# Seventeen bursts of score tiles in place of eighteen, and the last out product in two column halves

## The chip, the core and the metric

The kernel runs on one NeuronCore of a Trainium2 chip. Its engines run side by side, each through its own list of instructions in order: TensorE (PE; its weight loads are listed apart as PEld), VectorE (DVE), ScalarE (ACT), GpSimd (POOL) and SyncE (SP), which here only issues DMAs. Results of TensorE go to PSUM, eight banks of 512 f32 columns by 128 partitions. An engine that needs another's result, or a bank that another still reads, waits on a semaphore. The metric is the device time of one execution in microseconds; a lower one is better. The profile is of one execution, times in it are counted from the start of its span.

## What is computed

Attention with a sigmoid in place of the softmax, and behind it a two-layer network with the SiLU function. Inputs q, k and v have 8 batches, 12 heads, 448 rows and 64 columns; w_in is 768 x 2048, w_out 2048 x 768.

```python
scores = q @ k.T / sqrt(64) - log(448)
attn = sigmoid(scores) @ v            # for each batch and head
x = attn.transpose(0, 2, 1, 3).reshape(3584, 768)
h = x @ w_in
out = (h * sigmoid(h)) @ w_out        # 3584 x 768, float32
```

## The kernel before

**Groups and tiles.** Four heads of one batch make a group g, so a batch has three groups and there are 24. A group has seven score tiles (`scores`, L216): TensorE multiplies k and q into a double bank of PSUM (`psc`, four matmuls a tile), and ScalarE turns the 128 x 896 tile into `attnT` with one sigmoid (L230). When a group's seven tiles are through, `values` (L238) multiplies them with v on TensorE (28 matmuls into `pav`, L254), and VectorE moves the two results to `xT` (L265).

**Stages.** After a first stretch the program goes through pairs of batches, m = 0 to 3. For each pair there is a stage of out products (`sets`, L570: gTr, the hidden layer of pair m, times w_out) and a stage of hidden products for the next pair (`h_pair`, L360). Both use Strassen-like sums, seven products in place of eight. In the first three out stages the score tiles of pair m + 1 are put between the out products, 42 tiles (six groups) a stage; the fourth has none.

**An out set** (`out_set`, L485) makes two blocks of 128 rows: seven products of eight matmuls (384 columns each, L502), each into one bank `po` and then taken out by VectorE: L513, L517, L523, L526, L529, L534 with L535, L539 in that order. Sums of operands (`S`, L510 to L518) are VectorE's as well. The function is a generator and yields after each matmul; one yield is called a step here, so a product has eight steps and a set 56. In the eighth step of a product the instructions that take it out are issued. Stages m = 0 and 2 have three sets (168 steps), m = 1 and 3 four. Results are stored from `osb` with DMAs on SyncE's queue; in the last set of the program (`last`) the stores go by column halves, and some on ScalarE's queue: the left halves, then those on the right, two DMAs of 64 rows each.

**Banks.** In the first three out stages there are three double banks, taken in turn by score tiles and by `values` (L64 with 3), and two single ones for `po`. In the last stage, four single ones.

**The order of work in an out stage** is written out by hand (L765 to L786). A first number of steps is run (`FIRST_DENSE`), then a list of bursts: each has a size, the score tiles that it issues one after the other, and a count, the out steps that follow. With a burst's tiles goes one `values` if a group is complete (`burst`, L741). After the tiles, and once more in the middle of the count, `rows_if_any` (L589) puts in what waits for a place: a copy for the transpose of later q or k rows, with its DMA on SyncE's queue, or one of four sums of `xT` (`x_sums`, L343) that the hidden stage needs. At the end of the list the remaining steps of the stage run, ScalarE loads the SiLU table, and the hidden stage begins; its first two products stand ahead of the last group's `values`. At the start of an out stage ScalarE loads the sigmoid table (L771).

```python
FIRST_DENSE = 14
THREE_SETS = [(2, 8), (2, 9), (3, 13)] + [(2, 2), (2, 9), (3, 13)] * (2 * NQ - 1)
...
for size, count in bursts:
    burst(n, size)
    n += size
    rows_if_any(own, nc.vector.tensor_copy)
    for i in range(count):
        next(stream)
        if i == count // 2:
            rows_if_any(own, nc.vector.tensor_copy)
```

NQ is 3, so this list has 18 bursts: 42 tiles and 150 steps. With the 14 first ones 164 steps of 168 are through when it ends.

Of the kernel before, what the change touches and what calls it, by code (L numbers as in the profile page):

```python
# [17 lines left out]
def kernel(  # L18
# [9 lines left out]
    nc = tc.nc  # L28
# [8 lines left out]
    NQ = NPAIR // 2  # L37
# [3 lines left out]
    NO2 = DMODEL // 2  # L41
    NQB = NQ * B
    NHC = NFC // 2
# [20 lines left out]
    def banks_for_attention(doubles):  # L64
        psum.close()
        banks.clear()
        bufs_of.update(double=doubles, single=NBANK - 2 * doubles)
        for name, bufs in bufs_of.items():
            taken[name] = 0
            new_pool(name, bufs)  # L70
# [7 lines left out]
    def banks_for_h():  # L78
        doubles = [[2 * i, 2 * i + 1] for i in longest_idle("double")]
        ring[:] = sum(doubles[:-2], [])  # L80
        ring.extend(2 * bufs_of["double"] + i for i in longest_idle("single"))
        ring.extend(sum(doubles[-2:], []))
        psum.close()
        banks.clear()
        new_pool("any", 1)
        for i in range(NBANK):
            banks[i] = banks["any"].tile([P, 512], F32, tag=f"any{i}", name=f"any{i}")

    def one_bank(name):
        if "any" in banks:  # L90
            ring.append(ring.pop(0))
            return banks["any"].tile([P, 512], F32, tag=f"any{ring[-1]}", name=name)
        taken["single"] += 1
        return banks["single"].tile([P, 512], F32, tag="single", name=name)
# [265 lines left out]
    def h_pair(m, last_values):  # L360
# [97 lines left out]
    wq = [  # L458
        [w_out_sb[:, r * NHC : (r + 1) * NHC, c * NO2 : (c + 1) * NO2] for c in range(2)]
        for r in range(2)  # L460
    ]
# [23 lines left out]
    def out_set(a1, rows1, a2, rows2, last=False):  # L485
        lo, hi = slice(0, NHC), slice(NHC, NFC)
        osb = [p3.tile([P, DMODEL], F32, tag="osb", name="osb") for _ in range(2)]
        c11, c12 = (osb[0][:, nh * NO2 : (nh + 1) * NO2] for nh in range(2))
        c21, c22 = (osb[1][:, nh * NO2 : (nh + 1) * NO2] for nh in range(2))
        m1 = cpool.tile([P, NO2], F32, tag="m1", name="m1")  # L490
        sg = [cpool.tile([P, NHC, P], F16, tag=f"S{i}", name=f"S{i}") for i in range(1, 5)]

        def store(rows, o, cols, engines):
            for at, (row, eng) in enumerate(zip(rows, engines)):
                eng.dma_start(row[:, cols], o[at * HP : (at + 1) * HP, cols])

        left, right, whole = slice(0, NO2), slice(NO2, DMODEL), slice(0, DMODEL)

        def product(a, w):
            po = one_bank("po")  # L500
            for fc in range(NHC):
                nc.tensor.matmul(  # L502
                    po[:, :NO2], a[:, fc, :], w[:, fc, :], start=(fc == 0), stop=(fc == NHC - 1)
                )
                if fc < NHC - 1:
                    yield 163
            return po[:, :NO2]

        add, sub = nc.vector.tensor_add, nc.vector.tensor_sub
        add(sg[0], a2[:, lo], a2[:, hi])  # L510
        sub(sg[1], sg[0], a1[:, lo])
        po = yield from product(a1[:, lo], wq[0][0])
        (act_copy if last else nc.vector.tensor_copy)(m1, po)  # L513
        sub(sg[2], a1[:, lo], a2[:, lo])
        yield 163
        po = yield from product(a1[:, hi], wq[1][0])
        add(c11, po, m1)  # L517
        sub(sg[3], a1[:, hi], sg[1])  # L518
        if last:
            store(rows1, osb[0], left, (nc.sync, nc.sync))  # L520
        yield 163
        po = yield from product(sg[1], tw[2])
        add(c12, po, m1)  # L523
        yield 163
        po = yield from product(sg[2], tw[3])
        add(c22, po, c12)  # L526
        yield 163
        po = yield from product(a2[:, hi], tw[4])
        sub(c21, c22, po)  # L529
        if last:  # L530
            store(rows2, osb[1], left, (nc.sync, nc.scalar))
        yield 163
        po = yield from product(sg[0], tw[1])
        add(c22, po, c22)  # L534
        add(c12, po, c12)  # L535
        store(rows2, osb[1], right if last else whole, (nc.sync, nc.sync))
        yield 163
        po = yield from product(sg[3], wq[1][1])
        add(c12, po, c12)  # L539
        if last:  # L540
            store(rows1, osb[0], right, (nc.sync, nc.scalar))
        else:
            store(rows1, osb[0], whole, (nc.sync, nc.sync))
        yield 163

    by_h1 = {3: 6, 6: 7, 9: 8}
    early = [h_unit(0, fc) for fc in range(2)]
# [22 lines left out]
    def sets(m):  # L570
        for g in range(0, NCH - 1, 2):
            step = out_set(
                block(m, g), row_blocks(m, g), block(m, g + 1), row_blocks(m, g + 1)
            )
            for i, ns in enumerate(step):
                if m == 0 and g == 0 and i in (10, 14):
                    next(sums)
                if m == 0 and g == 0 and i in (20, 28, 36, 44):
                    next(in_sums)
                yield ns  # L580
        if m % 2 == 1:
            g = NCH - 1
            yield from out_set(
                kept, row_blocks(m - 1, g), block(m, g), row_blocks(m, g), m == B // 2 - 1
            )
# [3 lines left out]
    def rows_if_any(before, copy):  # L589
        if sums_of_x and next(sums_of_x[0], "end") == "end":  # L590
            sums_of_x.pop()
        if later and later[0][0] < before:
            g, name = later.pop(0)
            dma_transpose(g, name, copy)
            if name == "q":
                behind_rows(g, before)
# [49 lines left out]
    def after_values(g):  # L646
        if g == 0:
            load("v", 3)
            load_w_in(2)
            load_w_in(3)  # L650
        elif g == 1:
            load("v", 4)
            load_w_out(0, 0)
            load_w_out(0, 1)
        elif g == 2:
            load("v", 5)
            load_w_out(1, 0)
            load_w_out(1, 1)
            load("kq", 6)
            load("kq", 7)  # L660
        elif g + 3 < NQB:
            load("v", g + 3)
        if g >= 2 * NQ and g % (2 * NQ) == 2 * NQ - 2:
            sums_of_x.append(x_sums(g // (2 * NQ), 0, NQ - 1))
# [76 lines left out]
    def burst(n, size=2):  # L741

        new = units[n : n + size]
        for u in new:
            scores(*u)
        with_values = values_if_any()
        for g, ch in new:
            if ch == NCH - 1:
                waiting.append(g)
                if 9 <= g + 3 < NQB:  # L750
                    later.extend(((g + 3, "k"), (g + 3, "q")))
        return with_values
# [9 lines left out]
    for _ in stream:  # L762
        pass

    FIRST_DENSE = 14  # L765
    THREE_SETS = [(2, 8), (2, 9), (3, 13)] + [(2, 2), (2, 9), (3, 13)] * (2 * NQ - 1)
    FOUR_SETS = [(size, {2: 6, 3: 16}[size]) for size in (3, 3, 3, 2, 3, 2, 3, 3, 2, 3, 3, 2, 3, 2, 3)]
    FOUR_SETS.append((2, 10))
    for m in range(B // 2 - 1):
        banks_for_attention(3)  # L770
        nc.scalar.activation(warm, bias_s, AF.Sigmoid)  # L771
        stream = sets(m)
        for _ in range(FIRST_DENSE):
            next(stream)
        bursts = FOUR_SETS if m % 2 else THREE_SETS
        assert sum(size for size, _ in bursts) == 2 * NT_B
        own = 2 * NQ * (m + 2)
        n = 2 * NT_B * (m + 1)
# [8 lines that stand above are left out]
        assert not sums_of_x  # L787
        nc.scalar.activation(warm, bias_s, AF.Silu)
        for _ in stream:
            pass  # L790
        (g,) = waiting
        waiting.clear()
        banks_for_h()

        def last_values():
            values(g)
            after_values(g)
            for _ in x_sums(m + 1, NQ - 1, NQ):
                pass
            nc.gpsimd.tensor_copy(gate, tx[m + 1, 4][:1, NQ - 1, :1])  # L800

        for i, _ in enumerate(h_pair(m + 1, last_values)):
            if i % 8 == 7:
                rows_if_any(NQB, nc.gpsimd.tensor_copy)
# [33 lines left out]
```

## Time and profile before

| | us |
|---|---|
| time, median of 3 runs (lowest to highest) | 365.48 (365.35 to 365.48) |
| the profiled execution: its time | 365.46 |
| its span | 363.5 |
| out stage of m = 0 | 74.2 to 120.6 |
| out stage of m = 1 (four sets) | 154.0 to 209.6 |
| out stage of m = 2 | 242.8 to 289.2 |
| out stage of m = 3 (no score tiles) | 322.8 to the end |

The time is the span and what lies around it. Busy times of engines are sums of their instructions; matmul ends in the profile are modelled, so starts of matmuls are the better mark. The granted clock of TensorE is full from the first microseconds on. In the timeline a line gives start, length, engine, line of the program, what is written from what, and how many instructions are merged; in square brackets stands how long the engine was idle before it and for whom. "SPq" and "ACTq" are the queues on which these engines issue DMAs.

### The profile page before, as it was taken

The numbers are of one execution on the slowest core, as the hardware profiler recorded it, in microseconds if no ns is written. First come the engines' busy times: TensorE is split into PE (matmuls) and PEld (weight loads), VectorE is DVE, ScalarE is ACT, GpSimd is POOL, SyncE is SP. The second block draws the span as 40 slices with busy tenths as digits, with TensorE's granted clock in tenths as the row PEclk, the third lists the DMA queues.
The fourth block names the chain that finished last, engine by engine and source line by source line (L and its number), as shares of the span: only waits on it lengthen the run. The fifth ranks groups of instructions, "written<-read, shape, count | busy, mean of one in ns | idle before, by whom it ended". The sixth has DMA issues, their size and how long they took to land. (4 is left out here: it accounts for less than half of the span.)

```text
span 363.5 us, 7651 instructions
## 1 busy us (share of the span) xinstructions
PE 356.1 (98%) x3036; PEld 186.8 (51%) x3036; DVE 252.2 (69%) x459; ACT 249.3 (69%) x339; POOL 77.5 (21%) x116
## 2 busy tenths in 40 slices
PE   8999999999999999999999999999999999999995
PEld 6554445555555555555555455554555555556662
DVE  3565469787666587868566768795856677797763
ACT  5999886479989756688777746679899956640000
POOL 8666511040060272000033047000100000000000
PEclk9999999999999999999999999999999999999998
DMA  8999999979969599008679569802983120003333
GB/s 138 198 204 203 204 205 203 172 114 194 163 115 207 119 133 172 0 2 160 104 133 193 105 130 165 122 2 51 166 100 88 25 65 0 3 0 88 87 88 87
DMA packets 65859, 42.80 MB, mean 118 GB/s; under 512 B 36128, under 2 KB 62496, under 8 KB 65824
## 3 DMA queue, kind: packets, MB, share of 16 engines
q0 software_dynamic: 27072, 22.58, 42.6%
q1 hardware_dynamic: 38320, 19.34, 28.0%
q8 instruction: 24, 0.39, 0.5%
q10 hardware_dynamic: 432, 0.39, 0.3%
q14 instruction: 11, 0.09, 0.1%
HBM read 45.61 MB, written 11.01 MB: 156 GB/s over the span
## 5 line engine op out<-in xcount | busy, mean ns | idle before, releaser
L230 ACT ACTIVATE attnT<-psc,bias_s 128x896 f16<-128x896 f32 x168 | 157.9, 1009 | 20.6 <-PE psc L223 19.3
L502 PEld LDWEIGHTS <-S 128*128 128x128 f16 x448 | 42.0, 98 | 33.6 <-issue 8.1
L223 PE MATMUL psc<-qT,kT 64*64 64x448 f16 x672 | 48.9, 360 | 1.1 <-ACT attnT L230 0.8
L265 DVE TENSOR_SCALAR xT<-pav 128x448 f16<-128x448 f32 x48 | 27.7, 620 | 28.9 <-PE pav L254 28.9
L502 PEld LDWEIGHTS <-gTr 128*128 128x128 f16 x336 | 31.1, 98 | 27.3 <-issue 8.7
L124 POOL DMA_DIRECT2D vf<-in_v_dram x24 | 17.3, 723 | 129.7 <-PE pav L254 122.6
L502 PE MATMUL po<-w_out_sb,gTr 128*128 128x384 f16 x224 | 41.6, 327 | 0.0
L376 PEld LDWEIGHTS <-w_in_sb 128*128 128x128 f16 x288 | 27.9, 98 | 26.7 <-issue 1.1
L502 PE MATMUL po<-T,S 128*128 128x384 f16 x224 | 41.0, 327 | 0.0
L502 PE MATMUL po<-w_out_sb,S 128*128 128x384 f16 x224 | 40.8, 326 | 0.0
L286 PE MATMUL ph<-xT,w_in_sb 128*128 128x448 f16 x192 | 38.5, 353 | 0.0
L254 PE MATMUL pav<-attnT,vf 64*64 64x448 f16 x672 | 38.1, 351 | 0.1
L376 PE MATMUL pa<-xT,w_in_sb 128*128 128x448 f16 x144 | 33.2, 353 | 0.0
L223 PEld LDWEIGHTS <-kT 64*64 64x64 f16 x672 | 17.9, 104 | 27.8 <-issue 21.3
L376 PEld LDWEIGHTS <-SI 128*128 128x128 f16 x216 | 21.1, 98 | 20.0 <-issue 0.5
L254 PEld LDWEIGHTS <-vf 64*64 64x64 f16 x672 | 21.6, 106 | 12.3 <-issue 2.9
L286 PEld LDWEIGHTS <-w_in_sb 128*128 128x128 f16 x192 | 17.8, 98 | 18.9 <-issue 3.4
L392 ACT ACTIVATE part<-pa 128x448 f32<-128x448 f32 x24 | 12.7, 543 | 18.1 <-PE pa L376 18.1
L502 PE MATMUL po<-T,gTr 128*128 128x384 f16 x112 | 21.9, 327 | 0.6 <-DVE osb L523 0.6
L370 ACT ACTIVATE gTr<-pc 128x448 f16<-128x448 f32 x24 | 13.1, 544 | 12.9 <-DVE pc L386 12.5
L386 DVE TENSOR_TENSOR part<-pb,part 128x448 f32<-128x448 f32 x24 | 14.9, 622 | 8.3 <-ACT part L392 5.0
L184 ACT ACTIVATE m<-po 128x384 f32<-128x384 f32 x1 | 0.5, 491 | 27.3 <-PE po L502 27.3
(76 smaller groups left out, 471.1 us busy)
## 6 DMA issues: line engine op xcount, KB each, us to landing
out_dram<-osb SPq DMA_DIRECT2D x52, 192.0 KB, 3.2
vf<-in_v_dram POOLq DMA_DIRECT2D x24, 224.0 KB, 6.6
kf<-in_k_dram POOLq DMA_DIRECT2D x23, 224.0 KB, 7.4
qf<-in_q_dram POOLq DMA_DIRECT2D x23, 224.0 KB, 7.8
w_in_sb<-in_moe_w_in_dram POOLq DMA_DIRECT2D x16, 192.0 KB, 7.9
w_out_sb<-in_moe_w_out_dram POOLq DMA_DIRECT2D x4, 768.0 KB, 14.9
out_dram<-osb SPq DMA_DIRECT2D x6, 96.0 KB, 2.2
kT<-kr SPq DMA_TRANSPOSE x18, 5.1
```

What stands on the lines that cost most here:

```text
L124: nc.gpsimd.dma_start(flat[name, g][:, :, c0:c1].rearrange("p i c d -> p i (c d)"), rows_in(name, g)[:, :, c0 * D : c1 * D],)
L184: nc.scalar.activation(o, i, AF.Copy)
L223: nc.tensor.matmul(psc[own, j, :S], qkT["k", g][rows, ch, own], qkT["q", g][rows, :, own], start=True, stop=True,)
L230: nc.scalar.activation(attnT[g, ch], psc[:, :, :S], AF.Sigmoid, bias=bias_s, scale=QKSCALE)
L254: nc.tensor.matmul(pav[half][j * D : (j + 1) * D, :S], flat["v", g][own, j, ch, :], at[own, j, :], start=(ch == 0), stop=(ch == NCH - 1),)
L265: nc.vector.tensor_scalar_mul(xT[b][:, half * NQ + iq, :], pav[half][:, :S], SX)
L286: nc.tensor.matmul(ph[:, :S], w_in_sb[:, cc, fc * P : (fc + 1) * P], xT[b][:, cc, :], start=(at == 0), stop=(at == NCC - 1),)
L370: nc.scalar.activation(gTr[:, r * NG + i, col + c * S : col + (c + 1) * S], h, AF.Silu, bias=0.0, scale=ISX)
L376: nc.tensor.matmul(to, w[:, n, i * P : (i + 1) * P], x[:, n], start=(start and n == 0), skip_group_check=not start, stop=(n == NQ - 1),)
L386: nc.vector.tensor_add(o, po, x)
L392: nc.scalar.activation(got[i, 1], bank[i, "a"], AF.Copy)
L502: nc.tensor.matmul(po[:, :NO2], a[:, fc, :], w[:, fc, :], start=(fc == 0), stop=(fc == NHC - 1))
```

## The change

The stages of three sets (m = 0 and 2) get another list of bursts, and 13 first steps in place of 14. The first three bursts now have three tiles each with 13 steps behind; then come one of two (with the first `values`) and one of three, and from the fifteenth tile on the same three bursts are repeated as before. There are 17 bursts, 42 tiles and 154 steps in the list; with the 13 first ones 167 steps of 168. The stage of four sets (m = 1) is as it was.

In the last set of the program the seventh product (S4 times a quarter of w_out) is made in two halves of 192 columns, each with eight matmuls, a bank, an add and two stores of 64 rows x 192 columns, one on SyncE's and one on ScalarE's queue. Before, it was one product of 384 columns with one add and two stores of 64 x 384.

```diff
-        def product(a, w):
-            po = one_bank("po")
+        def product(a, w, cols=left):
+            po = one_bank("po")[:, : cols.stop - cols.start]
             for fc in range(NHC):
                 nc.tensor.matmul(
-                    po[:, :NO2], a[:, fc, :], w[:, fc, :], start=(fc == 0), stop=(fc == NHC - 1)
+                    po, a[:, fc, :], w[:, fc, cols], start=(fc == 0), stop=(fc == NHC - 1)
                 )
...
-        po = yield from product(sg[3], wq[1][1])
-        add(c12, po, c12)
-        if last:
-            store(rows1, osb[0], right, (nc.sync, nc.scalar))
-        else:
-            store(rows1, osb[0], whole, (nc.sync, nc.sync))
-        yield 163
+        pieces = 2 if last else 1
+        for at in range(pieces):
+            cols = slice(at * NO2 // pieces, (at + 1) * NO2 // pieces)
+            po = yield from product(sg[3], wq[1][1], cols)
+            add(c12[:, cols], po, c12[:, cols])
+            if last:
+                to = slice(NO2 + cols.start, NO2 + cols.stop)
+                store(rows1, osb[0], to, (nc.sync, nc.scalar))
+            else:
+                store(rows1, osb[0], whole, (nc.sync, nc.sync))
+            yield 163
...
-    FIRST_DENSE = 14
-    THREE_SETS = [(2, 8), (2, 9), (3, 13)] + [(2, 2), (2, 9), (3, 13)] * (2 * NQ - 1)
+    FIRST_DENSE = 13, 14
+    THREE_SETS = [(3, 13)] * 3 + [(2, 6), (3, 13)] + [(2, 2), (2, 9), (3, 13)] * (2 * NQ - 2)
...
-        for _ in range(FIRST_DENSE):
+        bursts = FOUR_SETS if m % 2 else THREE_SETS
+        for _ in range(FIRST_DENSE[m % 2]):
             next(stream)
-        bursts = FOUR_SETS if m % 2 else THREE_SETS
```

More of the change, by code (lines that the diff above doesn't have):

```diff
@@ L506, in product @@
                     yield 163
-            return po[:, :NO2]
+            return po
         add, sub = nc.vector.tensor_add, nc.vector.tensor_sub
```

## The prediction

> **What bounds the kernel now.** I read the page's shares first, then the chain that ended last, then the timelines of ScalarE, VectorE and SyncE at the places that the change touches.
>
> ```profile
> span 363.5 us, 7651 instructions
> PE 356.1 (98%) x3036; PEld 186.8 (51%) x3036; DVE 252.2 (69%) x459; ACT 249.3 (69%) x339; POOL 77.5 (21%) x116
> PEclk9999999999999999999999999999999999999998
> ```
>
> TensorE works all the time at the full granted clock, so only two things help: fewer TensorE microseconds, or a shorter end behind its last matmul. Prices come from the chain, which in the stages before 359 us consists of TensorE pieces alone (start, length, what):
>
> ```profile
> 247.67 1.57 PE po L502 x9
> 249.24 0.69 PE psc L223 x12
> 249.94 2.22 PE po L502 x13
> 252.15 0.50 PE psc L223 x8
> ...
> 322.76 36.41 PE po L502 x224
> ```
>
> The last line has nothing but out steps: 36.41 / 224 = 0.1625 us a step. A stretch of 13 steps takes 2.22, that is 2.11 and 0.11 over. A burst of two score tiles (8 matmuls) takes 0.50, one of three (12) takes 0.69: a tile costs 0.19, and 0.12 is fixed. So breaking the out steps for a burst costs 0.12 + 0.11 = 0.23 us beyond its tiles.
>
> **Bursts: what is removed.** The stages of three sets are those from 74.2 and 242.8 us (m = 0 and 2). Tiles (42), out steps (168) and value products (5, all behind bursts of two, as before) stay the same; bursts go from 18 to 17. That is one break less a stage: 2 x -0.23 = -0.46 us. No DMA and no copy is added; the copies and x sums that follow bursts (`rows_if_any`) slide by a few steps. The key rows kT and qT of the group that the third burst now reaches early (tiles 7 and 8) were transposed in the stage before in both cases (SyncE's transposes for m = 2 run from 215.9 to 228.4), so nothing new is waited for there.
>
> **Bursts: what is given back at the start.** Three tiles use all three double banks, so the third tile of a burst waits until ScalarE has read the third tile of the burst before.
>
> ```profile
> 244.32 1.28 ACT L771 ACT_TABLE_LOAD   x1
> ...
> 245.73 3.78 ACT L230 ACTIVATE attnT<-psc,bias_s 128x896 f16<-128x896 f32 x4
> ```
> ```profile
> 117.49 2.81 ACT L230 ACTIVATE attnT<-psc,bias_s 128x896 f16<-128x896 f32 x3 [0.17 <-PE psc L223]
> ```
>
> Three sigmoids in a row take 2.81: about 0.905 apart, 1.00 the last. Two bursts of three lie 0.69 + 2.22 = 2.91 apart, so ScalarE keeps pace once it has started in time. At m = 2 it doesn't: the first burst stood at 245.19 after 14 steps and moves to 245.03, but the sigmoid table is loaded until 245.60 and the first sigmoid starts at 245.73 whatever TensorE does. Its third ends at 245.73 + 2.81 = 248.54. The next burst starts at 245.03 + 2.91 = 247.94 and its third tile 0.38 later, at 248.32; with 0.05 from a reader's end to the next writer (117.96 to 118.01 below) it waits 0.27. I take 0.25. ScalarE has caught up by the third burst. At m = 0 the table is there at 76.46 and the first burst comes at 76.40, its sigmoids 0.44 later: third end 76.84 + 2.81 = 79.65, third tile of the next burst 76.40 + 2.91 + 0.38 = 79.69. Margin 0.04, cost 0. Behind TensorE's stall every engine's work merely slides.
>
> **Bursts: what is given back at the end.** The page's lines do not show that VectorE already makes TensorE wait near the end of these stages; its timeline does (m = 0):
>
> ```profile
> 114.61 1.16 DVE L265 TENSOR_SCALAR xT<-pav 128x448 f16<-128x448 f32 x2 [1.99 <-PE pav L254]
> 115.68 0.62 DVE L355 TENSOR_TENSOR tx<-xT 128x896 f16<-128x896 f16 x1
> 116.33 0.62 DVE L355 TENSOR_TENSOR tx<-xT,tx 128x896 f16<-128x896 f16 x1
> 116.88 0.62 DVE L355 TENSOR_TENSOR xT<-xT 128x896 f16<-128x896 f16 x1
> 117.41 0.55 DVE L526 TENSOR_TENSOR osb<-po,osb 128x384 f32<-128x384 f32 x1
> 117.88 0.61 DVE L355 TENSOR_TENSOR tx<-xT,tx 128x896 f16<-128x896 f16 x1
> 118.41 0.55 DVE L529 TENSOR_TENSOR osb<-osb,po 128x384 f32<-128x384 f32 x1
> ```
> ```profile
> 118.01 2.76 PE L502 MATMUL po<-w_out_sb,S 128*128 128x384 f16 x16
> ```
>
> There are two single banks for out products, so the sixth product of the last set waits for the eviction of the fourth (L526), which ends at 117.96; the step before it stands at 117.69, so 0.32 passes where 0.17 is usual: 0.15 lost. With the change the last value burst is put before step 143, the last of that fourth product, instead of before step 140. The order of VectorE's instructions becomes two xT, one x sum, L526, then the other three x sums, L529. From the start of the value products: xT at 1.57 (113.05 to 114.61), then 0.54, 0.53 and 0.53 to L526, which ends at 3.72; the bank is free at 3.77. TensorE: values 1.45, two steps and a break 0.43, two tiles 0.50, and the seven steps 145 to 151 to 3.53. Wait 0.24 instead of 0.15. L529 then starts after 0.47 + 3 x 0.53 and ends at 5.78, free 5.83; its bank is wanted at 5.87: no wait, by 0.04. So +0.09 a stage, +0.19 for both. Bounds: 0 to 0.72 a stage for the wait itself, since the stage of four sets loses 0.72 to the same clump (L523 behind three x sums, TensorE held until 204.90). I take the worked 0.24, as intervals between the same operations give it. The sigmoids end about 0.3 after the stage's last step instead of before it; the value product that needs them comes 1.23 later, and ScalarE's next load and copies had 1.4 us of idle time (122.69 to 124.13), so this is hidden.
>
> **The last product in halves.** Before:
>
> ```profile
> 358.38 0.55 DVE L535 TENSOR_TENSOR osb<-po,osb 128x384 f32<-128x384 f32 x1
> 358.49 1.77 SPq L495 DMA_DIRECT2D out_dram<-osb  x3
> 359.20 0.56 DVE L539 TENSOR_TENSOR osb<-po,osb 128x384 f32<-128x384 f32 x1 [0.28 <-PE po L502]
> 359.79 0.50 ACTq L495 DMA_DIRECT2D out_dram<-osb  x1
> ```
> ```profile
> SPq L833 <- DMA out_dram<-osb: 1.9, 1, 1.9
> ```
>
> The last add ends at 359.76, both queues issue at 359.79, the stores land at 362.2, and 1.3 us of closing steps follow. TensorE: 448 columns take 0.189 a step, 384 take 0.1625, so 0.00041 a column, and 192 columns 0.083; 16 x 0.083 = 1.33 against 1.30, +0.03. (Weight loads of 0.098 are hidden behind matmuls that start 0.060 apart in the warm start-up products at 6.4 us.) VectorE: 448 columns 0.625, 384 columns 0.557, so a half takes 0.35. The first half can start at 358.85 behind L535 and ends at 359.20; the second runs 359.22 to 359.57, 0.19 earlier than before. ScalarE's queue issues the first store at 359.23 for 0.50 and so the second at 359.78: as before. SyncE still has the two stores of the other row block, until 359.59; its third issue can't start before 359.70 and its fourth not before 360.25 to 360.33, half a microsecond later than the single one before. Against that, a store of 48 KB has half the bytes: the last 96 KB one had its packets on the way for 0.67 us, so 0.33 less. Landing 2.2 - 0.33 = 1.9 after 360.3 is 362.2, no gain. In closing, SyncE goes through eight DMA semaphores 0.06 apart; the store that landed last was first in that order and will be fourth, so up to 0.18 of these steps fall before the landing. I take -0.10; bounds -0.30 (half of the queue's delay away as well) and +0.35 (the next paragraph).
>
> **Sum.** -0.46 + 0.25 + 0.19 - 0.10 = -0.12. The profiled run took 365.46 for its span of 363.5 (1.9 around it), 0.02 from the median of 365.48. 365.46 - 0.12 = 365.3.
>
> **The rivals.**
> (1) Clean saving: the two waits don't grow. -0.46 - 0.10 = -0.56: 364.9. For it: the margins are tenths. Against: the table load's end and VectorE's order are fixed by the program.
> (2) A store costs the same whatever its size: 64 packets of 768 bytes take as long as 64 of 1536. Then SyncE's fourth landing comes 0.33 later: tail +0.23, 365.7. For it: every store has 64 packets. Against: in the packet records the 768-byte packets at the very start took 0.036 each and 1536-byte ones on the same queue 0.065. The Trainium skill, "DMA: Bandwidth & Descriptors", section Bandwidth (Measured), speaks for this one: "Transfers under 64 KB are descriptor-dominated", and this change makes four stores of 48 KB of two of 96. By that rule alone the forecast would be 365.7; the packet times of this trace go against it.
> (3) Other side: ScalarE doesn't keep pace in the run of three bursts of three. It decides where the sigmoid's pitch passes 0.97 (2.91 / 3). At its mean duration of 1.009 the third tile of the second burst waits 79.92 - 79.69 = 0.23 at m = 0 and 0.49 at m = 2, and the third burst 0.12 more in each: 0.96 in place of 0.25, so 366.0. Against: 2.81 for three.
> (4) VectorE's clump costs 0.72 in each stage as in the four-set one: (0.72 - 0.24) x 2 = +0.96, 366.3. Against: L526 now has one x sum ahead of it, not three.
>
> **How the numbers follow.** Chances: the sum 0.52, (1) 0.15, (2) 0.14, (3) 0.11, (4) 0.08. The time is 365.3. The range reaches from just under (1) to (3), 364.8 to 366.0, and leaves out (4) and the outer parts of (1) and (3). About 0.2% (0.73 us: 364.75 and 366.21) is what a measurement of this kernel can tell from no change: beyond it lies below a part of (1) with the lower edge of the sum, 0.09; above it most of (4) and a little of (3), 0.10; within 0.81.
>
> **What would show it.** Right: TensorE's stages from 74.2 and 242.8 some 0.14 shorter and 0.1 longer or equal; a wait of a quarter microsecond in the middle of the second burst at m = 2; L526 behind one x sum and a wait of 0.24 after it; four SyncE issues in a row until 360.8; the last landing near 362.2. Wrong: a second wait at L529, waits at m = 0's second burst, ScalarE's sigmoids more than 0.95 apart, or a last landing after 362.4. A change of more than 0.73 either way would mean that a wait that I priced in tenths is another one altogether.

## The result and the profile after

| | before | changed |
|---|---|---|
| time, median of 13 runs each, us | 365.35 | 366.10 |
| lowest to highest | 364.87 to 365.63 | 365.65 to 367.31 |
| ratio of the times, 95% interval | | 1.0026, 1.0015 to 1.0037 |
| profiled execution: time, span | 365.46, 363.5 | 366.39, 364.3 |

The changed kernel is slower by 0.26%, 0.95 us (0.55 to 1.35 by the interval; the medians are 0.75 apart, the means 0.95). The page looks as before: TensorE is busy for 356.3 us, 98% of the span.

Most of what was foretold is there. TensorE's timeline at the end of the stage of m = 0 (start, length, engine, line, what, how many; in brackets the idle time before and its releaser):

```profile
115.86 1.31 PE L502 MATMUL po<-T,gTr 128*128 128x384 f16 x7
117.25 0.48 PE L502 MATMUL po<-w_out_sb,S 128*128 128x384 f16 x2
117.67 0.76 PE L223 MATMUL psc<-qT,kT 64*64 64x448 f16 x12
118.36 2.45 PE L502 MATMUL po<-w_out_sb,S 128*128 128x384 f16 x14
121.02 1.29 PE L376 MATMUL pa<-xT,w_in_sb 128*128 128x448 f16 x6 [0.21 <-ACT attnT L230]
```

The gap between 115.86 + 7 steps (117.00) and 117.25 is the eviction's wait, 0.24 by unrounded starts. The last line is what was not foretold: fourteen steps from 118.36 on are through at 120.65, but the first hidden product starts at 121.02, and it is released by ScalarE's sigmoid (L230). Idle time in the brackets is counted from the modelled end of the last matmul and so is smaller than the loss; from matmul start to matmul start 0.53 pass where 0.16 is usual, so 0.37 is lost. ScalarE's timeline:

```profile
118.16 2.80 ACT L230 ACTIVATE attnT<-psc,bias_s 128x896 f16<-128x896 f32 x3 [0.40 <-PE psc L223]
120.98 1.28 ACT L792 ACT_TABLE_LOAD   x1
```

The last three sigmoids end at 120.97. The hidden product starts 0.05 later. In the kernel before, the same three started at 117.49 and were through at 120.30, and the first hidden product stood at 120.61, one step behind the last out product:

```profile
120.61 0.35 PE L376 MATMUL pa<-xT,w_in_sb 128*128 128x448 f16 x1
```

So the same dependence was there and had 0.26 to spare: 120.30 and 0.05 is 120.35. At m = 2 the chain that ended last was, before, TensorE alone

```profile
286.33 3.02 PE po L502 x17
289.35 1.14 PE pa L376 x6
```

and now goes through ScalarE:

```profile
287.60 0.57 issue
288.17 1.91 ACT attnT L230 x2
290.07 0.04 issue
290.12 1.29 PE pa L376 x6
```

VectorE's order is the foretold one, L526 behind one x sum:

```profile
115.05 1.16 DVE L265 TENSOR_SCALAR xT<-pav 128x448 f16<-128x448 f32 x2 [2.47 <-PE pav L254]
116.12 0.61 DVE L355 TENSOR_TENSOR tx<-xT 128x896 f16<-128x896 f16 x1
116.65 0.55 DVE L526 TENSOR_TENSOR osb<-po,osb 128x384 f32<-128x384 f32 x1
...
118.72 0.55 DVE L529 TENSOR_TENSOR osb<-osb,po 128x384 f32<-128x384 f32 x1
```

So is the third tile at m = 2, in TensorE's and in ScalarE's timeline. The second burst of three is 1.01 long and the first 0.76. In starts, the third tile comes 0.22 late, and from the burst's start to the next out step 0.94 pass (248.35 to 249.29) in place of 0.69 (245.44 to 246.13): 0.25, as foretold.

```profile
245.44 0.76 PE L223 MATMUL psc<-qT,kT 64*64 64x448 f16 x12
...
248.35 1.01 PE L223 MATMUL psc<-qT,kT 64*64 64x448 f16 x12
```
```profile
244.73 1.28 ACT L775 ACT_TABLE_LOAD   x1
...
246.13 4.58 ACT L230 ACTIVATE attnT<-psc,bias_s 128x896 f16<-128x896 f32 x5
```

Five sigmoids take 4.58 without an idle gap: 0.9 apart, the pace that the prediction took from three in a row. At the end of the program SyncE issues five stores and ScalarE three from 358.1 on, and the half stores land faster (issues of the last 5 us; size, median time to landing):

```profile
out_dram<-osb SPq DMA_DIRECT2D x2, 96.0 KB, 2.1
out_dram<-osb ACTq DMA_DIRECT2D x2, 48.0 KB, 2.0
out_dram<-osb SPq DMA_DIRECT2D x2, 48.0 KB, 1.9
```

Single times scatter by a microsecond, more than the terms in question. The trace lets one go round this: the distance between the first matmuls of two stages is the same in all profiles to 0.02 us when nothing is changed there (hidden stages 33.41 or 33.42, the stage of m = 1 55.38 or 55.39, so that before it ran from 154.0 to 209.4; the 209.6 in the table of times before is 0.2 too late). All the scatter of the ten profiles lies in the first stretch, which ended between 73.67 and 75.45, and there ahead of the first value product, which began between 15.10 and 16.86; from that one to the first out step 58.51 to 58.59 pass in all ten. What delays it was not looked into. So each experiment below is read from the stages of its one profile, with the repeated times beside them. In microseconds; the last column is the same at m = 0 and m = 2:

| kernel | first stretch | out stage m = 0 | out stage m = 2 | last stage to the end | step to first hidden product |
|---|---|---|---|---|---|
| before | 74.20 | 46.41 | 46.36 | 40.92 | 0.16 |
| changed | 74.38 | 46.64 | 46.89 | 40.81 | 0.53 |
| e1_idle_bank | 74.38 | 46.27 | 46.52 | 41.06 | 0.16 |
| e2_before_idle_bank | 73.86 | 46.41 | 46.36 | 41.15 | 0.16 |
| e3_bursts_only | 73.69 | 46.64 | 46.88 | 40.91 | 0.53 |
| e4_halves_only | 73.94 | 46.40 | 46.35 | 40.81 | 0.16 |
| e7_one_bank | 75.45 | 46.29 | 46.54 | 40.81 | 0.16 |
| e6_first14 | 73.94 | 46.56 | 46.65 | 40.84 | 0.66 |
| e5_first14_one_bank | 73.67 | 46.06 | 46.15 | 40.82 | 0.16 |
| e8_first14_queues | 74.36 | 46.06 | 46.14 | 40.83 | 0.16 |

Changed against before, by stages: +0.23 + 0.53 - 0.11 = +0.65; 0.18 more of the profiled difference is the first stretch.

### The profile page after: what moved, and what is told of

It is laid out like the page before. It is cut to its first block, busy times and chain, and to the rows that moved or that the text cites. A ratio compares the mean times of both kernels' runs of the same rounds, so it can differ in the third digit from the quotient of the medians.

```text
span 364.3 us, 7670 instructions
## 1 busy us (share of the span) xinstructions
PE 356.3 (98%) x3044; PEld 187.4 (51%) x3044; DVE 250.9 (69%) x460; ACT 248.7 (68%) x339; POOL 77.5 (21%) x116
## 5 line engine op out<-in xcount | busy, mean ns | idle before, releaser
L230 ACT ACTIVATE attnT<-psc,bias_s 128x896 f16<-128x896 f32 x168 | 157.5, 1008 | 22.4 <-PE psc L223 21.1
L502 PE MATMUL po<-w_out_sb,S 128*128 128x384 f16 (+1 forms) x232 | 40.8, 321 | 0.2
L124 POOL DMA_DIRECT2D kf<-in_k_dram x25 | 18.2, 726 | 5.5 <-DMA vf<-in_v_dram 1.4
```

The costliest lines, as they stand in the source:

```text
L124: nc.gpsimd.dma_start(flat[name, g][:, :, c0:c1].rearrange("p i c d -> p i (c d)"), rows_in(name, g)[:, :, c0 * D : c1 * D],)
L230: nc.scalar.activation(attnT[g, ch], psc[:, :, :S], AF.Sigmoid, bias=bias_s, scale=QKSCALE)
L502: nc.tensor.matmul(po, a[:, fc, :], w[:, fc, cols], start=(fc == 0), stop=(fc == NHC - 1))
```

## The experiments

**Whose bank is it?** The hidden stage uses all eight banks in a list that `banks_for_h` makes from the order in which the score tiles took the double banks, the longest idle one first. It takes the order to be 0, 2, 4 (first bank of each double). In the built program the tiles go through them as 0, 4, 2, and its list of PSUM addresses shows the last score tile and the first hidden product (`pa`) both in bank 4. So the stage begins with the bank that is busy longest. The traces show no bank numbers; what bears this out is what the exchanges of banks below do to the wait. The first run puts that right:

```diff
-        doubles = [[2 * i, 2 * i + 1] for i in longest_idle("double")]
+        n = bufs_of["double"]
+        doubles = [[2 * (-i % n), 2 * (-i % n) + 1] for i in longest_idle("double")]
```

> The changed kernel, with the banks of the hidden stage listed in the order in which the score tiles really left them (double banks 0, 4, 2 are taken in turn, not 0, 2, 4), so that its first product takes the double bank that has been free longest. Theory A (the first hidden product waits for the last sigmoid because it is given that sigmoid's bank; 0.35 us in each of the two stages): that wait goes, the stages from m = 0 and m = 2 become 0.35 shorter each, the time 0.70 below the changed kernel's, so 0.2 below the kernel before. Rival B (the sigmoids as such are late, and the hidden stage would wait for them at the next place, the value product of the last group): the 0.35 turn up again within the next 3 us, and the time stays 0.75 above before. Rival C (the loss is the start of the program, which was 0.19 later in the profile of the changed kernel, and other scatter): no change against the changed kernel.

365.44 against 365.30 for the kernel before on the same chip, ratio 1.0003 (0.9990 to 1.0015); the changed kernel, which was not run again beside it, had 1.0026. The wait is gone from both stages, each 0.37 shorter than in the changed kernel:

```profile
118.36 2.45 PE L503 MATMUL po<-w_out_sb,S 128*128 128x384 f16 x14
120.64 1.30 PE L377 MATMUL pa<-xT,w_in_sb 128*128 128x448 f16 x6
```

The stages behind are 33.41 as ever, so B falls: the lateness does not turn up again. C falls too, as the first stretch was the same, 74.38, in this profile and in the changed kernel's. But the last stage got longer by 0.25. There the second out product takes bank 3, and with the whole list exchanged that bank held the very last hidden result: ScalarE's last SiLU ended at 324.27, and the ninth step came at 324.32, 0.40 after the eighth. The run with one exchange below tests this.

> The kernel before with the same corrected order of banks and nothing else. Theory A: there the last sigmoid ended 0.31 ahead of the first hidden product, so the wrong bank cost nothing; 0.0 against before, within 0.2. If the order of banks helps by itself elsewhere in the hidden stage (rival to A's reading of the first run): faster than before by as much as the first run gained on the changed kernel, 0.7.

365.48 against 365.30, 1.0002 (0.9990 to 1.0013). The stages of m = 0 and m = 2 are the same as before to 0.01: the wrong bank cost the kernel before nothing. Only the new wait in the last stage is there, +0.23.

**Which half of the change?**

```diff
-        pieces = 2 if last else 1
+        pieces = 1
```

> The new list of bursts with the last product in one piece as before. Theory A: the whole loss lies in the bursts: 0.70 for the bank, 0.25 for the third tile at m = 2, 0.16 for the eviction, less 0.46 for the two breaks, is +0.65 against before (the tail's gain of 0.11 is missing). If the halves were what costs: 0.0 to -0.2 against before.

366.06 against 365.30, 1.0016 (1.0005 to 1.0026). The stages are those of the changed kernel and the last one that of before. By stages this is +0.74 against before, a little over the 0.65 expected. The loss is in the bursts.

```diff
-    FIRST_DENSE = 13, 14
-    THREE_SETS = [(3, 13)] * 3 + [(2, 6), (3, 13)] + [(2, 2), (2, 9), (3, 13)] * (2 * NQ - 2)
+    FIRST_DENSE = 14, 14
+    THREE_SETS = [(2, 8), (2, 9), (3, 13)] + [(2, 2), (2, 9), (3, 13)] * (2 * NQ - 1)
```

> The old list of bursts with the last product in halves. By the profile of the changed kernel the stretch from the last product's first matmul to the end is 5.71 us against 5.83: -0.11 against before. If the halves are what costs (a queue of four issues on SyncE, the last one at 0.54 later): +0.3 or more, and the stretch above 6.1 us.

365.21 against 365.30, 0.9998 (0.9985 to 1.0011): a tenth cannot be told in the times. The trace has it: 40.81 in place of 40.92.

**The bank alone, and a dose of the wait.** One exchange, 4 and 2, is enough; bank 5 is wanted 0.57 later, when the last sigmoid is through, and bank 3 stays where it was.

```diff
         ring.extend(sum(doubles[-2:], []))
+        if bufs_of["double"] == 3:
+            ring[0], ring[6] = ring[6], ring[0]
```

> The changed kernel with two banks exchanged in the list of the hidden stage, 4 and 2 (the first product takes bank 2, that of the first tile of the last burst; bank 5 stays second, bank 3 stays last). In the first run all of 4, 5 and 2, 3 changed places, and the last out stage got a new wait of 0.23 us in its second product, because its bank 3 was then the last one that ScalarE read. Theory A: no 0.37 in the two stages and no 0.23 in the last one: stages of 46.27 and 46.52, from the last stage's start to the end 40.81, sum 0.70 below the changed kernel, 0.1 below before. If the 0.23 stays, the bank was not its cause: 41.05 from the last stage's start.

365.24 against 365.36, 0.9994 (0.9980 to 1.0007). 46.29, 46.54 and 40.81: the 0.37 are gone and the 0.23 did not come. By stages -0.12 + 0.18 - 0.11 = -0.05 against before, which a measurement cannot tell from nothing.

```diff
-    FIRST_DENSE = 13, 14
+    FIRST_DENSE = 14, 14
```

> The changed kernel with 14 first steps in place of 13 in the stages of three sets, banks as in the changed kernel. One step later are all bursts, and so the last sigmoid, against the end of the stage. Theory A: the first hidden product waits 0.16 longer, 0.53 in place of 0.37, in each of the two stages. By the same placing of rows as in the prediction the eviction's wait of 0.24 goes in both (the fourth product's last matmul now stands ahead of the value burst, so its add is not behind the xT), and the third tile at m = 2 waits 0.08 in place of 0.23: stages about 46.5 and 46.6, sum -0.4 against the changed kernel. Rival: if the first hidden product's wait had another cause than the last sigmoid, it would stay 0.37.

365.69 against 365.36, 1.0003 (0.9989 to 1.0017). The gap at the first hidden product grew from 0.53 to 0.66, so the wait from 0.37 to 0.50, a little less than the one step of 0.16, because an eviction behind the last burst still holds TensorE up by 0.03. The timelines of TensorE and of ScalarE at m = 0:

```profile
117.85 2.31 PE L502 MATMUL po<-w_out_sb,S 128*128 128x384 f16 x13
120.50 1.29 PE L376 MATMUL pa<-xT,w_in_sb 128*128 128x448 f16 x6 [0.34 <-ACT attnT L230]
```
```profile
117.65 2.80 ACT L230 ACTIVATE attnT<-psc,bias_s 128x896 f16<-128x896 f32 x3 [0.17 <-PE psc L223]
```

The sigmoids end at 120.45 and again the product follows 0.05 later. The third tile at m = 2 now starts 0.06 late in place of 0.22, and the next out step 0.08 in place of 0.25: a step later, a step less. The two stages are 0.08 and 0.24 shorter than the changed kernel's, together 0.32 where 0.4 was expected.

**Both together.** The changed kernel with 14 first steps and the one exchange of banks:

> 14 first steps and the two banks exchanged. Theory A: all three waits (bank, eviction, third tile but for 0.08) gone: stages about 46.0 and 46.1, the last stage to the end 40.81, so 0.8 below before. Rival: a wait that is taken away here comes up at the next place, and the sum is less than -0.4.

364.58 against 365.36, 0.9978 (0.9964 to 0.9993): faster than the kernel before. The changed kernel was not run beside it; by stages it takes 1.31 longer. 46.06, 46.15 and 40.82 are -0.35, -0.21 and -0.10 against before, -0.66. That is a little less than the 0.8 expected: the stages are 0.06 and 0.05 longer than placed, of which an eviction's wait of 0.03 in each is seen in the trace.

```profile
117.57 2.31 PE L504 MATMUL po<-w_out_sb,S 128*128 128x384 f16 x13
119.73 1.30 PE L378 MATMUL pa<-xT,w_in_sb 128*128 128x448 f16 x6
```

**SyncE's queue at the end.** On top of that:

```diff
-        store(rows2, osb[1], right if last else whole, (nc.sync, nc.sync))
+        store(rows2, osb[1], right if last else whole, (nc.sync, nc.scalar if last else nc.sync))
```

> As the run before, and in the last set one of the two stores that SyncE issues ahead of the halves goes to ScalarE's queue, so each queue has three issues, not four and two. If SyncE's queue is what holds the last store (issued 0.54 later than in the kernel before, after a wait of only 0.05 behind the third): its fourth issue, now the third, comes 0.6 earlier, and the stretch from the last stage's start to the end is 40.4 to 40.6 in place of 40.81. If the time of the landing itself decides: 40.81 still.

364.78 against 365.36, 0.9975 (0.9963 to 0.9987): not to be told from the run before. The last stage took 40.83, so this exchange gained nothing. Issues in the last 5 us:

```profile
out_dram<-osb SPq DMA_DIRECT2D x2, 48.0 KB, 1.9
out_dram<-osb ACTq DMA_DIRECT2D x2, 48.0 KB, 2.2
```

SyncE's last store was issued and landed 0.4 earlier against the end than in the changed kernel. But ScalarE's last store, issued at the same moment as there, took 2.2 to land in place of 2.0, and it lands last. The two last issues are now 0.04 apart, where they were 0.34 apart. So the run does not show that SyncE's queue did not hold the end before; it shows that what was won on one queue was lost on the other.

## Why the prediction was wrong

**The step that failed** is the one at the end of the stages: "The sigmoids end about 0.3 after the stage's last step instead of before it; the value product that needs them comes 1.23 later ... so this is hidden." The lateness was right (0.32: 120.97 against 120.65). The cover was named for the wrong reader: not only the value product waits for the last sigmoid, but also the first product of the hidden stage, which needs its bank. It stands right behind the last step, with no cover at all, and the kernel before had 0.26 to spare there. Cost: 0.37 a stage, 0.74 in all. With it the sum of the prediction is -0.12 + 0.74 = +0.62, 366.1, and the trace has +0.65. The prediction followed the data that pass between engines over the end of the stage, and the banks only inside it. None of the rivals was this one.

**The other terms, by the trace.** A break less is worth 0.23, with 0.02 left over: the stage of m = 0 in the run with one bank exchanged is 46.29, and 46.41 - 0.23 + 0.09 is 46.27. The eviction's wait is 0.24 as worked out, and TensorE did not wait for L529. The third tile costs the 0.25 at m = 2 and nothing at m = 0. The stage of m = 2 has 0.06 more that was in no term: the value bursts run in two ways, 1.83 or 1.89 from burst to next step, and one more than before was of the slower kind. The halves bring -0.11 for -0.10. Counted from the start of the last stage, the last landing came at 39.65 in place of 39.58, so no earlier, as foretold; what was gained is the closing behind it, 1.16 in place of 1.34, the 0.18 of the prediction. One step inside was off: the first half's add began 0.10 after L535's end and not right behind it, so VectorE was done 0.11 earlier and not 0.19.

**The rivals.** The measured 366.1 lies near the times of (3) and (4), 366.0 and 366.3, but by chance: neither of their waits was there. Three bursts of three in a row did not let ScalarE fall behind, 4.58 for five. With one x sum ahead of L526 the clump cost 0.24, not 0.72. The store of 48 KB was not as dear as that of 96: packets of 768 bytes took 0.036 on SyncE's queue and 0.052 on ScalarE's (medians) where those of 1536 took 0.112 and 0.065. SyncE's last store had its packets on the way for 0.36 in place of 0.67, and landed 1.92 after its issue in place of 2.16; so it got cheaper by 0.24 of the 0.33 that half the bytes were to bring, and most of the time to landing did not go with the size. The rule of the Trainium skill, "DMA: Bandwidth & Descriptors", section Bandwidth, under "Measured", that transfers under 64 KB are descriptor-dominated, would by the prediction's terms have put the end of the last stage 0.33 later. The trace does not bear that out for this step from 96 to 48: the end came at 40.81.

## What to carry to other kernels

When work is moved towards the end of a stage, look for every reader of what it leaves late: the buffers that the next stage takes over count as much as its data. Where one engine is busy for 98% of the time, losing a margin of a quarter microsecond can cost more than the change gains. Ask of the built program in which order buffers are really handed out; a list that assumes the order can be wrong without cost, as here before the change, and then take away the gain of the next one. Where times scatter more than the effect, distances between stages within the trace can still settle it.

## What the runs showed of the hardware

When both queues issued a store of the same size within 0.005 us of each other, the one on ScalarE's queue landed later: 2.4 us after its issue against 2.2 for 96 KB (kernel before), 2.1 against 1.9 for 48 KB (the first halves in the last run). With the issues 0.3 apart (changed kernel, 48 KB) it was 2.0 against 1.9. Why is not shown. Small out products of 192 columns, each with its own weight load, ran 0.0825 apart, about half of the 0.1625 for 384, with no sign of the weight loads. Changing from out steps to score tiles and back cost 0.23 us each time, for bursts of two tiles and of three alike.
